# Attention by pairs of heads: q and k of two heads in one 128-row tile, scores as 64-row products on the two halves of the array

## The chip, the core and the metric

The kernel runs on one core of a Trainium2 chip. The core has a matrix engine (TensorE, PE in the profile, with its weight loads as PEld), a vector engine (VectorE, DVE), a scalar engine (ScalarE, ACT), a general engine (GpSimd, POOL) and a queue processor that starts transfers (SyncE, SP). The metric is the device time of one launch in microseconds (us); lower is better. Matmuls read two operands from the on-chip memory (SBUF): the weights (lhsT), which are loaded into the array, and the moving operand (rhs), which streams through it column by column; the result goes to PSUM, eight banks of 128 partitions x 512 fp32 values.

## The reference

Three stages run one behind the other on 1,792 tokens (4 batches x 448) with 768 features: causal attention with 12 heads of 64 per batch, a top-1 mixture of 8 experts (768 to 1024 to 768, ReLU), and a second feed-forward layer (768 to 2048 to 768 with h - tanh(h)). The part that matters here:

```
q, k, v: (4, 12, 448, 64) fp32
scores = (q @ k.T) / sqrt(64)
scores = where(causal mask, -1e9, scores)
scores = scores - max(scores, axis=-1)
attn   = exp(scores);  attn /= sum(attn, axis=-1) + 1e-9
out    = attn @ v                       # then (1792, 768)
expert = argmax(x @ w_gate); x -> prob * (relu(x @ w1[expert]) @ w2[expert])
x -> (h - tanh(h)) @ w_out, h = x @ w_in
```

## The kernel before

The attention works through 48 heads (4 batches x 12), the loop `for n in range(NHEAD + 2)` at L632. Products that need more precision than one pass in the 32-bit format fp32r gives are made from parts: x = hi + lo, where hi is x rounded to fp32r and lo the rest.

For each head three 128-row operand tiles and one tile of 65 rows exist. `q1` holds q hi in rows 0 to 63 and q lo in rows 64 to 127; `k1` holds k hi twice; `q2` holds q hi and, in row 64, minus the row maximum; `k2` holds k lo and a row of ones. So `k1` by `q1` is k hi (q hi + q lo) in one product of 128 rows, and `k2` by `q2` adds k lo q hi and subtracts the row maximum in one product of 65 rows (`attend`, L552 and L553). Scores come out with keys on partitions, in four blocks of 128 keys and 448, 320, 192 and 64 queries (the causal part). ACT takes the exponent (L554) into `pT`, POOL zeroes the half above the diagonal (L555).

The row maximum has to be known first. `rowmax` (L528) makes approximate scores with queries on partitions, again four blocks of up to 128 queries and 64 to 448 keys, and DVE takes mask and maximum in one instruction (L530, with a second, short one that reads the accumulator). `maxrow` (L540, L541) turns the four columns of maxima into a row of `q2`.

`turn` (L455, L459) turns q or k of two heads at once on PE (128 rows: the two heads), and ACT writes each head's half as hi; `turn_lo` (L468) makes lo on DVE, one instruction per head; `turn_dup` (L475) makes the second copies on ACT. `weigh` (L567) is the product with v in full fp32 (two records a call), `output` (L585 to L599) turns the result back and divides by the sum of the weights. Between these, `cv` converts blocks of the last layer's weights for later (L108 to L132: ACT, POOL, three DVE instructions, POOL), `pick`, `rank` and `choose` do the gate of a batch that is complete, and near the end `fetch0` and `gather` fetch the first expert's tokens.

Each engine runs its instructions in the order in which the loop writes them. Scores and maxima have two PSUM banks each (`ps_s`, `ps_a`), turned tiles two (`ps_t`), `pv` and `po` one each. The first head is handled apart by `begin` (L477). After the attention the experts start with L799.

Of the kernel before, what the change touches and what calls it, by code (L numbers as in the profile page):

```python
# [27 lines left out]
def fused_kernel(ctx, tc, q, k, v, wg, w1, w2, win, wout, out):  # L28
# [6 lines left out]
    CP = 112  # L35
# [168 lines left out]
    ps_a = ectx.enter_context(tc.tile_pool(name="ps_a", bufs=2, space=PSUM))  # L204
    ps_s = ectx.enter_context(tc.tile_pool(name="ps_s", bufs=2, space=PSUM))
# [162 lines left out]
    with ExitStack() as actx:  # L368
# [3 lines left out]
        xsp = actx.enter_context(tc.tile_pool(name="xsp", bufs=2))  # L372
        ps_p = actx.enter_context(tc.tile_pool(name="ps_p", bufs=1, space=PSUM))
        NQ = 7
# [7 lines left out]
        raw_t, ops_t, max_t, pt_t, ov_t, xs, tn_t = {}, {}, {}, {}, {}, {}, {}  # L382

        k2s = [ap1.tile([D + 1, S], F32R, name=f"k2_{i}") for i in range(NQ)]
        vs = [ap1.tile([KP, NKB, 2, D + 1], F32, name=f"v_{i}") for i in range(NV)]

# [9 lines left out]
        def load_v(i):  # L396
            b, hp = divmod(i, NP)
            v_sb = vs[i % NV]
            nf = S // KP
            for j in range(2):  # L400
                nc.sync.dma_start(out=v_sb[:, 0:nf, j, 0:D],
                                  in_=v[b, 2 * hp + j, 0:nf * KP].rearrange("(c p) d -> p c d", p=KP))
            if S % KP:
                nc.sync.dma_start(out=v_sb[0:S % KP, nf, :, 0:D],
                                  in_=v[b, 2 * hp:2 * hp + 2, nf * KP:].rearrange("j p d -> p j d"))
# [6 lines left out]
        load_qk(0)  # L412
        load_qk(1)
# [4 lines left out]
        mcs = [ap1.tile([KP, NKB], F32R, name=f"mcol{i}") for i in range(3)]  # L418
        pts = [ap1.tile([KP, NKB, S], F32, name=f"pT{i}") for i in range(2)]
        junk = ap1.tile([KP, S], BF16, name="junk")  # L420
        for t in k2s:
            nc.gpsimd.memset(t[D:D + 1].bitcast(F32), 1.0)
        for t in vs:
            nc.gpsimd.memset(t[:, :, :, D:D + 1], 1.0)
            if S % KP:
                nc.gpsimd.memset(t[S % KP:, NKB - 1], 0.0)
        for t in mcs:
            nc.gpsimd.memset(t.bitcast(F32), 0.0)
        for t in pts:
            if S % KP:  # L430
                nc.gpsimd.memset(t[S % KP:, NKB - 1, S - S % KP:], 0.0)
# [7 lines left out]
        def turn(i, z, pool=ps_t, tag="tp"):  # L439
            if i >= NPAIR:  # L440
                return
            q_sb, k_sb = raw_t[i]
            if z:
                for j in range(2):
                    n = 2 * i + j
                    q1 = ap2.tile([128, S], F32R, tag="q1", name="q1", bufs=NQ)
                    k1 = ap2.tile([128, S], F32R, tag="k1", name="k1", bufs=NQ)
                    q2 = ap2.tile([D + 1, S], F32R, tag="q2", name="q2", bufs=NQ)
                    ops_t[n] = (q1, k1, q2, k2s[n % NQ])
# [3 lines left out]
            pt = pool.tile([128, S], F32, tag=tag, name="tp")  # L453
# [3 lines left out]
            for j in range(2):  # L457
                q1, k1, q2, k2 = ops_t[2 * i + j]
                nc.scalar.copy(out=(k1 if z else q1)[0:D], in_=pt[j * D:(j + 1) * D])  # L459
            tn_t[i, z] = pt  # L460

        def turn_lo(i, z):
            if (i, z) not in tn_t:
                return
            pt = tn_t.pop((i, z))
            for j in range(2):
                q1, k1, q2, k2 = ops_t[2 * i + j]
                nc.vector.tensor_tensor(out=k2[0:D] if z else q1[D:], in0=pt[j * D:(j + 1) * D],  # L468
                                        in1=(k1 if z else q1)[0:D].bitcast(F32), op=ALU.subtract)

        def turn_dup(i, z, j):
            if i >= NPAIR:
                return
            q1, k1, q2, k2 = ops_t[2 * i + j]
            nc.scalar.copy(out=k1[D:] if z else q2[0:D], in_=(k1 if z else q1)[0:D].bitcast(F32))  # L475

        def begin():  # L477
            q_sb, k_sb = raw_t[0]
            pts = {}
            for j in range(2):  # L480
                for z, src in ((1, k_sb), (0, q_sb)):
                    pool, tag = (ps_p, ("po", "pv")[z]) if j else (ps_t, "tp")
                    pt = pool.tile([128, S], F32, tag=tag, name="pt0")
                    for c in range(NCH):
                        nc.tensor.transpose(pt[0:D, c * CP:(c + 1) * CP], src[:, c, j, :], ident[:CP, :CP])
                    pts[j, z] = pt[0:D]
                q1 = ap2.tile([128, S], F32R, tag="q1", name="q1", bufs=NQ)
                k1 = ap2.tile([128, S], F32R, tag="k1", name="k1", bufs=NQ)
                q2 = ap2.tile([D + 1, S], F32R, tag="q2", name="q2", bufs=NQ)
                ops_t[j] = (q1, k1, q2, k2s[j])  # L490
            raw_t.pop(0)
            for j in range(2):
                q1, k1, q2, k2 = ops_t[j]
                nc.scalar.copy(out=k1[0:D], in_=pts[j, 1])
                nc.vector.tensor_copy(k1[D:], k1[0:D].bitcast(F32))
                nc.scalar.copy(out=q1[0:D], in_=pts[j, 0])
                nc.vector.tensor_tensor(out=q1[D:], in0=pts[j, 0], in1=q1[0:D].bitcast(F32), op=ALU.subtract)
                if j == 0:
                    nc.scalar.copy(out=q2[0:D], in_=q1[0:D].bitcast(F32))
# [698 lines left out]
```

## Time and profile before

| | |
|---|---|
| time, median of 3 runs | 1141.39 us (1140.04 to 1143.49) |
| profiled execution | 1140.54 us, span from first to last instruction 1139.1 us |
| busy: PE, PEld, DVE, ACT, POOL | 95%, 86%, 69%, 57%, 37% of the span |
| attention | from 0 to about 291.8 us, where the first expert product starts |
| attention, 22.23 to 281.03 us | PE busy 236.27, DVE 228.19, ACT 214.38, POOL 129.62 of 258.80 us |

Busy time of a matmul counts from its start to the modelled end of its result, so neighbouring matmuls overlap in it; the distance between their starts says more on what one costs. An idle stretch has the instruction that ended it behind an arrow. A tile's name is that of the program, without the number: the tiles `q1`, `q2`, `k1`, `k2` all appear as q and k.

### The profile page before, as it was taken

To read this page: it belongs to the slowest core of one execution; us is meant where nothing else is said; L and a number is where in the kernel's file an instruction comes from. 1 tells how busy PE (TensorE), PEld (TensorE's weight loads), DVE (VectorE), ACT (ScalarE), POOL (GpSimd) and SP (SyncE) were. 2 spreads that over 40 slices of the span, in tenths; PEclk is the share of its full clock that TensorE was granted. 3 is DMA by queue.
4 is the path that set the end of the run, shared out by engine and by line. 5 is a ranking of instruction groups with operands and counts; after the bars stand their busy time and mean duration, and the time that the engine had idled before them with its cause. 6 is when DMAs were issued, how large, how long until landed. Compare 5 with 4: busy or idle time off the path is not lost. (4 is left out here: it accounts for less than half of the span.)

```text
span 1139.1 us, 22520 instructions
## 1 busy us (share of the span) xinstructions
PE 1077.2 (95%) x7019; PEld 980.6 (86%) x7019; DVE 782.7 (69%) x1958; ACT 649.6 (57%) x1415; POOL 417.1 (37%) x740
## 2 busy tenths in 40 slices
PE   6999899989899999998999899999999999999996
PEld 4676676766789888988889899999999999999996
DVE  5888999997822444617565599889999865556653
ACT  5888888887422544627565565555567634434442
POOL 5555454543314101011102245657674322222221
PEclk8999999999999999999999999999999999999999
DMA  7677676755451557718878353444656422331310
GB/s 154 169 192 178 171 171 164 176 132 159 147 153 43 174 165 245 250 57 283 261 250 289 127 190 132 132 159 164 206 178 230 167 85 83 111 105 64 112 52 33
DMA packets 151044, 179.75 MB, mean 158 GB/s; under 512 B 75392, under 2 KB 119936, under 8 KB 149120
## 3 DMA queue, kind: packets, MB, share of 16 engines
q1 hardware_dynamic: 144656, 148.30, 43.4%
q0 software_dynamic: 6256, 29.90, 7.9%
q8 instruction: 57, 0.93, 0.3%
q14 instruction: 75, 0.61, 0.2%
HBM read 263.49 MB, written 46.80 MB: 272 GB/s over the span
## 5 line engine op out<-in xcount | busy, mean ns | idle before, releaser
L1032 PE MATMUL ph<-yt,w1hi 128*128 128x256 f32 x1344 | 260.4, 284 | 3.4 <-ACTq L973 3.4
L1069 PE MATMUL po<-w2hi,gg 128*128 128x384 f32 x896 | 248.1, 338 | 2.3 <-DVE gg L151 2.3
L1032 PEld LDWEIGHTS ph<-yt,w1hi 128*128 128x128 f32 x1344 | 217.7, 192 | 3.7 <-ACTq L973 3.7
L1032 PE MATMUL ph<-yt,w1lo 128*128 128x256 f32 x672 | 190.5, 283 | 0.0
L1069 PEld LDWEIGHTS po<-w2hi,gg 128*128 128x128 f32 x896 | 164.2, 189 | 2.6 <-DVE gg L151 2.6
L1069 PE MATMUL po<-w2lo,gg 128*128 128x384 f32 x448 | 150.3, 336 | 0.0
L799 PE MATMUL ph<-w1hi,xt 128*128 128x512 f32 x432 | 145.0, 403 | 0.0
L1032 PEld LDWEIGHTS ph<-yt,w1lo 128*128 128x128 f32 x672 | 128.8, 192 | 0.0
L1050 DVE SCALAR_TENSOR_TENSOR g<-sq,g 128x256 f32<-128x256 f32 x224 | 111.4, 497 | 11.6
L567 PE MATMUL pv<-pT,v 128*65 128x64 f32 (+3 forms) x384 | 111.3, 391 | 0.2 <-POOL pT L555 0.2
L528 PE MATMUL pa<-k,q 128*128 128x448 f32 x192 | 88.9, 465 | 23.3 <-DVE q L468 17.9
L819 PE MATMUL py<-w2hi,hhi 128*128 128x384 f32 x288 | 100.7, 350 | 1.6 <-ACT hhi L149 1.6
L819 PE MATMUL py<-w2hi,hlo 128*128 128x384 f32 x288 | 98.2, 341 | 1.3 <-DVE hlo L151 1.3
L819 PE MATMUL py<-w2lo,hhi 128*128 128x384 f32 x288 | 97.8, 340 | 0.0
L799 PEld LDWEIGHTS ph<-w1hi,xt 128*128 128x128 f32 x432 | 82.7, 191 | 17.5
L530 DVE CUSTOM_DVE_ANT_0 junk<-pa,maskf 128x448 bf16<-128x448 f32 x192 | 80.2, 418 | 24.5 <-PE pa L528 6.5
L151 DVE TENSOR_TENSOR hlo<-tp,hhi 128x512 fp32r<-128x512 f32 x36 | 24.8, 689 | 104.0 <-ACTq L778 99.4
L109 POOL TENSOR_SCALAR cv_m<-cv_m 128x256 f32<-128x256 f32 (+3 forms) x82 | 83.1, 1013 | 28.2 <-ACT cv_m L108 23.1
L151 DVE TENSOR_TENSOR w2lo<-raw,w2hi 128x1536 fp32r<-128x1536 f32 x40 | 69.7, 1760 | 33.3 <-ACT w2hi L149 33.1
L528 PEld LDWEIGHTS pa<-k,q 128*128 128x128 f32 x192 | 35.1, 184 | 62.7 <-DVE q L468 26.2
L151 DVE TENSOR_TENSOR w1lo<-raw,w1hi 128x1536 fp32r<-128x1536 f32 (+1 forms) x47 | 68.6, 1480 | 26.2 <-ACT w1hi L149 25.3
L799 PE MATMUL ph<-w1lo,xt 128*128 128x512 f32 x216 | 86.1, 399 | 0.0
(675 smaller groups left out, 2340.6 us busy)
## 6 DMA issues: line engine op xcount, KB each, us to landing
raw<-in_moe_w_dram SPq DMA_DIRECT2D x148, 768.0 KB
raw<-win_dr POOLq DMA_DIRECT2D x72, 768.0 KB
raw<-wout_dr POOLq DMA_DIRECT2D x17, 768.0 KB
yt_dr<-yt SPq DMA_DIRECT2D x7, 1536.0 KB
yt<-yt_dr SPq DMA_DIRECT2D x7, 1536.0 KB
y_dr<-ysb POOLq DMA_DIRECT2D x18, 384.0 KB
cv_raw<-in_moe_w_out_dram SPq DMA_DIRECT2D x24, 256.0 KB
cv_raw<-in_moe_w_in_dram SPq DMA_DIRECT2D x24, 256.0 KB
```

What stands on the lines that cost most here:

```text
L109: nc.gpsimd.tensor_scalar(out=m, in0=m, scalar1=TINY * TINY, scalar2=None, op0=ALU.is_ge)
L151: eng.tensor_tensor(out=dlo, in0=src, in1=dhi.bitcast(F32), op=ALU.subtract)
L528: nc.tensor.matmul(pa[:nq, :w], lhsT=q1[:, q0:w], rhs=k1[:, :w], start=True, stop=True)
L530: nc.vector.tensor_tensor_reduce(out=junk[:nq, :w], in0=pa[:nq, :w], in1=maskf[:nq, m0:m0 + w], scale=1.0, scalar=-3.0e38, op0=ALU.add, op ...
L567: nc.tensor.matmul(pv[:, k0:], lhsT=vs[(n // 2) % NV][:, kb, n % 2, :], rhs=pt_t[n][:, kb, k0:], start=(kb == 0), stop=(kb == NKB - 1))
L799: nc.tensor.matmul(ph, lhsT=a[:, kk, :], rhs=w[:, kk, z * 512:(z + 1) * 512], start=(kk == 0 and n_ == 0), stop=(kk == KD - 1 and n_ == 2))
L819: nc.tensor.matmul(pys[z], lhsT=a[:, kk, :], rhs=w[:, kk, z * HALF:(z + 1) * HALF], start=(kk == 0 and n_ == 0), stop=(kk == KF - 1 and n_ ...
L1032: nc.tensor.matmul(ph, lhsT=w[:, kk, f * 128:(f + 1) * 128], rhs=yt[:, a, kk, :], start=(kk == 0 and n_ == 0), stop=(kk == KD - 1 and n_ = ...
L1050: nc.vector.scalar_tensor_tensor(out=g, in0=sq, scalar=float(c_), in1=g, op0=ALU.add, op1=ALU.mult)
L1069: nc.tensor.matmul(po_t[ub][tt][z], lhsT=gg[:, a, tt * 128:(tt + 1) * 128], rhs=w[:, f, z * HALF:(z + 1) * HALF], start=(f == 0 and n_ == ...
```

## The change

Two heads become one unit, a pair. `turn` still turns two heads at once, but its 128 rows (head 0 in rows 0 to 63, head 1 in rows 64 to 127) are kept as they are: ACT writes `qhi` or `khi` in one instruction, `turn_lo` writes `qlo` or `klo` in one, and `turn_dup`, `q1`, `q2`, `k1`, `k2` are gone. `half(t, j)` is head j's 64 rows of a tile. The scores of a block of keys are four products of 64 rows for each head: k hi q hi, k hi q lo, k lo q hi, and `one` by `mrow`, which subtracts the maximum; the two heads' products stand next to each other, one on rows 0 to 63 and one on rows 64 to 127, and write to two PSUM banks of one tile `ps`. `rowmax` is q hi by k hi alone, two products of 64 rows. One exponent and one mask instruction then do both heads. `ps` and `pa` are now one buffer of two banks each. The last block's weights are 128 columns, of which 64 are wanted (before 64). `maxrow` is done once for a pair. The start has no `begin`: it turns the first three pairs and takes the maxima of the first two before the loop, whose body is written out anew for a pair; what the loop did at head n (conversion, gate, fetches) is in `convert(n)` and `events(n)`.

```diff
-    ps_a = ectx.enter_context(tc.tile_pool(name="ps_a", bufs=2, space=PSUM))
-    ps_s = ectx.enter_context(tc.tile_pool(name="ps_s", bufs=2, space=PSUM))
...
+        ps_c = actx.enter_context(tc.tile_pool(name="ps_c", bufs=1, space=PSUM))
...
+        one = ap1.tile([KP, KP], F32R, name="one")
+        nc.vector.memset(one.bitcast(F32), 0.0)
+        for j in range(2):
+            nc.vector.memset(one[j * D:j * D + 1].bitcast(F32), 1.0)
...
-            for j in range(2):
-                q1, k1, q2, k2 = ops_t[2 * i + j]
-                nc.scalar.copy(out=(k1 if z else q1)[0:D], in_=pt[j * D:(j + 1) * D])
+            nc.scalar.copy(out=ops_t[i][2 * z], in_=pt)
...
-                nc.vector.tensor_tensor(out=k2[0:D] if z else q1[D:], in0=pt[j * D:(j + 1) * D],
-                                        in1=(k1 if z else q1)[0:D].bitcast(F32), op=ALU.subtract)
-
-        def turn_dup(i, z, j):
+            hi, lo = ops_t[i][2 * z:2 * z + 2]
+            nc.vector.tensor_tensor(out=lo, in0=tn_t.pop((i, z)), in1=hi.bitcast(F32), op=ALU.subtract)
+
+        def half(t, j):
+            return t[j * D:(j + 1) * D]
...
-            nc.tensor.matmul(pa[:nq, :w], lhsT=q1[:, q0:w], rhs=k1[:, :w], start=True, stop=True)
+            pa = ps_c.tile([KP, 2, 512], F32, tag="pa", name="pa")
+            for j in range(2):
+                nc.tensor.matmul(pa[:, j, :w], lhsT=half(qhi, j)[:, q0:q0 + KP], rhs=half(khi, j)[:, :w],
+                                 start=True, stop=True)
...
-            nc.tensor.matmul(ps[:nk, k0:], lhsT=k1[:, k0:k0 + nk], rhs=q1[:, k0:], start=True, stop=False)
-            nc.tensor.matmul(ps[:nk, k0:], lhsT=k2[:, k0:k0 + nk], rhs=q2[:, k0:], start=False, stop=True)
-            nc.scalar.activation(out=pT[:nk, kb, k0:], in_=ps[:nk, k0:], func=AF.Exp, scale=0.125)
+            w, o = S - k0, KO[kb]
+            p0, kk = KP - nk, k0 + nk - KP
+            ps = ps_c.tile([KP, 2, 512], F32, tag="ps", name="ps")
+            for n_, (a, m) in enumerate(((khi, qhi), (khi, qlo), (klo, qhi), (one, mrs[i % 2]))):
+                ks = slice(0, KP) if a is one else slice(kk, kk + KP)
+                for j in range(2):
+                    nc.tensor.matmul(ps[:, j, :w], lhsT=half(a, j)[:, ks], rhs=half(m, j)[:, k0:],
+                                     start=(n_ == 0), stop=(n_ == 3))
+            nc.scalar.activation(out=pT[p0:, :, o:o + w], in_=ps[p0:, :, :w], func=AF.Exp, scale=0.125)
...
+        for p in range(NPAIR + 2):
+            last = 2 * (p - 1)
+            attend(p, 0)
+            rowmax(p + 2, 3)
+            weigh(last, 0)
+            weigh(last, 1)
+            convert(2 * p)
+            attend(p, 1)
+            rowmax(p + 2, 2)
+            weigh(last, 2)
+            weigh(last, 3)
+            output(last - 1)
+            maxrow(p + 1)
+            events(2 * p)
+            attend(p, 2)
+            rowmax(p + 2, 1)
+            weigh(last + 1, 0)
+            weigh(last + 1, 1)
+            turn(p + 3, 1)
+            convert(2 * p + 1)
+            turn_lo(p + 3, 1)
+            attend(p, 3)
+            rowmax(p + 2, 0)
+            weigh(last + 1, 2)
+            weigh(last + 1, 3)
+            output(last)
+            turn(p + 3, 0)
+            turn_lo(p + 3, 0)
```

On PE, in the middle of the attention, the matmuls of one head stood so before (ps: scores, pa: approximate scores, pm: maxima turned, pv: product with v; the shape is that of the result; x4 is four instructions in a row):

```order
L552 MATMUL ps<-q_1424,k_1425 128x448
L553 MATMUL ps<-q_1426,k_3_178 128x448
L528 MATMUL pa<-k_1598,q_1597 128x448
L552 MATMUL ps<-q_1424,k_1425 128x320
L553 MATMUL ps<-q_1426,k_3_178 128x320
L540 MATMUL pm<-identr,mcol_205 1x128 x4
L567 MATMUL pv<-pT_208,v_184 65x448
L528 MATMUL pa<-k_1598,q_1597 128x320
L552 MATMUL ps<-q_1424,k_1425 128x192
L553 MATMUL ps<-q_1426,k_3_178 128x192
L552 MATMUL ps<-q_1424,k_1425 64x64
L553 MATMUL ps<-q_1426,k_3_178 64x64
```

In the change the same place holds, for two heads, four score products and one approximate product for each width, each twice (x2: the two halves), with the product with v behind each block:

```order
L503 MATMUL ps<-qhi,khi 128x448 x2
L503 MATMUL ps<-qlo,khi 128x448 x2
L503 MATMUL ps<-qhi,klo 128x448 x2
L503 MATMUL ps<-mrow_182,one 128x448 x2
L475 MATMUL pa<-khi,qhi 128x448 x2
L517 MATMUL pv<-pT_179,v_175 65x448
L517 MATMUL pv<-pT_179,v_175 65x320
L503 MATMUL ps<-qhi,khi 128x320 x2
L503 MATMUL ps<-qlo,khi 128x320 x2
L503 MATMUL ps<-qhi,klo 128x320 x2
L503 MATMUL ps<-mrow_182,one 128x320 x2
L475 MATMUL pa<-khi,qhi 128x320 x2
```

So for a width two heads took four score products and two approximate ones before, and take eight and two now, all of them of 64 rows.

On DVE, at the end of a head, the maxima (ISA), the lo parts (L468) and the output stood so before (mcol: columns of maxima; rs, x_sb, tl: output):

```order
L530 ISA junk,mcol_206<-pa,maskf 128x192
L530 ISA mcol_206 128x1
L530 ISA junk,mcol_206<-pa,maskf 64x64
L530 ISA mcol_206 64x1
L468 TENSOR_TENSOR q_2326<-tp,q_2326 64x448
L468 TENSOR_TENSOR q_2329<-tp,q_2329 64x448
L587 TENSOR_SCALAR rs<-po 112x4
L588 RECIPROCAL rs<-rs 112x4
L590 TENSOR_TENSOR x_sb<-po,rs 112x4x64
L598 TENSOR_TENSOR tl<-po,rs 112x32
L530 ISA junk,mcol_206<-pa,maskf 128x448
```

At the end of a pair in the change:

```order
L462 TENSOR_TENSOR klo<-tp,khi 128x448
L479 ISA junk,mcol_181<-pa,maskf 64x64
L479 ISA mcol_181 64x1
L479 ISA junk,mcol_181<-pa,maskf 64x64
L479 ISA mcol_181 64x1
L536 TENSOR_SCALAR rs<-po 112x4
L537 RECIPROCAL rs<-rs 112x4
L539 TENSOR_TENSOR x_sb<-po,rs 112x4x64
L547 TENSOR_TENSOR tl<-po,rs 112x32
L462 TENSOR_TENSOR qlo<-tp,qhi 128x448
L479 ISA junk,mcol_180<-pa,maskf 128x448
```

The lo parts of a pair are two instructions of 128 rows where there were four of 64; the maxima and the output are as many as before, the maxima of the two heads now side by side.

At the start of the program PE of the change turns pairs and takes maxima before the first score product (tp: turned q or k):

```order
L453 MATMUL tp<-ident,q_sb 128x112 x4
L475 MATMUL pa<-khi,qhi 128x448 x2
L475 MATMUL pa<-khi,qhi 128x320 x2
L475 MATMUL pa<-khi,qhi 128x192 x2
L475 MATMUL pa<-khi,qhi 128x64 x2
L488 MATMUL pm<-identr,mcol_180 65x128 x4
L453 MATMUL tp<-ident,k_sb 128x112 x4
L453 MATMUL tp<-ident,q_sb 128x112 x4
L503 MATMUL ps<-qhi,khi 128x448 x2
```

These rows begin with the q of the second pair; the k and q of the first pair and its four pairs of maxima stand ahead of them. Before, the first score product stood behind the first head's four maxima.

## Rows read from the trace of the kernel before

**Rows 1.** Stretches: length, busy PE, PEld, DVE, ACT, POOL, granted clock, DMA share, GB/s.
```profile
22.23:281.03 258.80, 236.27 (x1661) 179.44 (x1661) 228.19 (x830) 214.38 (x501) 129.62 (x305) 0.97 0.67 168
149.87:160.49 10.62, 9.77 (x76) 7.74 (x74) 9.47 (x37) 9.33 (x23) 5.66 (x15) 1.00 0.64 171
160.49:170.93 10.44, 9.78 (x76) 7.82 (x74) 9.49 (x34) 9.33 (x23) 5.09 (x13) 1.00 0.73 181
```

**Rows 2.** Timeline of DVE: start, duration, engine, line, operation.
```profile
155.46 1.28 DVE L468 TENSOR_TENSOR q<-tp,q 64x448 fp32r<-64x448 f32 x2
156.76 0.16 DVE L587 TENSOR_SCALAR rs<-po 112x4 f32<-112x4 f32 x1
...
157.61 0.61 DVE L530 CUSTOM_DVE_ANT_0 junk<-pa,maskf 128x448 bf16<-128x448 f32 x1
```

**Rows 3.** Waits from 100 to 200 us: total, times, longest.
```profile
PE pa L528 <- DVE q L468: 6.2, 8, 1.0
```

**Rows 4.** Timeline of PE, two heads from 149.87 us.
```profile
149.87 0.45 PE L552 MATMUL ps<-q,k 128*128 128x448 f32 x1
150.16 0.36 PE L553 MATMUL ps<-q,k 65*128 65x448 f32 x1
150.36 0.37 PE L528 MATMUL pa<-k,q 128*128 128x448 f32 x1
150.57 0.31 PE L552 MATMUL ps<-q,k 128*128 128x320 f32 x1
150.72 0.31 PE L553 MATMUL ps<-q,k 65*128 65x320 f32 x1
150.87 0.41 PE L540 MATMUL pm<-identr,mcol 128*1 128x128 f32 x4
151.11 0.92 PE L567 MATMUL pv<-pT,v 128*65 128x448 f32 x2
...
152.02 0.26 PE L552 MATMUL ps<-q,k 128*128 128x192 f32 x1
152.11 0.27 PE L553 MATMUL ps<-q,k 65*128 65x192 f32 x1
152.22 0.20 PE L552 MATMUL ps<-q,k 128*64 128x64 f32 x1
152.25 0.22 PE L553 MATMUL ps<-q,k 65*64 65x64 f32 x1
152.30 0.60 PE L455 MATMUL tp<-ident,q_sb 112*128 112x112 f32 x4
...
154.63 0.45 PE L552 MATMUL ps<-q,k 128*128 128x448 f32 x1
...
156.13 0.47 PE L528 MATMUL pa<-k,q 128*128 128x448 f32 x1 [0.85 <-DVE q L468]
```

**Rows 5.** Groups of DVE and ACT by shape, 100 to 200 us: busy, mean ns, idle before.
```profile
L468 DVE TENSOR_TENSOR k<-tp,k 64x448 fp32r<-64x448 f32 x18 | 11.1, 618 | 0.2
L475 ACT CAST k<-k 64x448 fp32r<-64x448 f32 x18 | 9.3, 561 | 0.2
L554 ACT ACTIVATE pT<-ps 128x448 f32<-128x448 f32 x17 | 9.2, 541 | 1.4 <-PE ps L553 1.1
L554 ACT ACTIVATE pT<-ps 64x64 f32<-64x64 f32 x18 | 3.7, 208 | 0.0
```

**Rows 6.** Timeline of PE, start of the program.
```profile
5.72 0.95 PE L485 MATMUL pt<-ident,q_sb 112*64 112x112 f32 x4
...
22.23 0.72 PE L552 MATMUL ps<-q,k 128*128 128x448 f32 x1
```

**Rows 7.** Timeline of PE, end of the attention.
```profile
276.84 0.45 PE L552 MATMUL ps<-q,k 128*128 128x448 f32 x1
...
290.46 0.72 PE L232 MATMUL tp<-identr,xg 128*128 128x128 f32 x6 [2.73 <-DMA xg<-x_dr,idx]
...
291.79 0.48 PE L799 MATMUL ph<-w1hi,xt 128*128 128x512 f32 x1
```

More of the change, by code (lines that the diff above doesn't have):

```diff
@@ L410, in load @@
                 load_v(i)
-        load_qk(0)
-        load_qk(1)
+        for i in range(3):
+            load_qk(i)
         maskf = ap1.tile([KP, S], BF16, name="maskf")
@@ L437, in fused_kernel, with turn @@
         nc.gpsimd.memset(zrow, 0.0)
-        def turn(i, z, pool=ps_t, tag="tp"):
-            if i >= NPAIR:
+        def turn(i, z):
+            if not 0 <= i < NPAIR:
                 return
@@ L477, in begin @@
[L477 to L499, printed above, removed]
-                    for c in range(NKB - 1, -1, -1):
-                        rowmax(0, c)
-                nc.vector.tensor_tensor(out=k2[0:D], in0=pts[j, 1], in1=k1[0:D].bitcast(F32), op=ALU.subtract)
-            maxrow(0)
-            nc.scalar.copy(out=q2[0:D], in_=q1[0:D].bitcast(F32))
-            turn(1, 1)
-            turn_dup(1, 1, 0)
-            turn_dup(1, 1, 1)
-            for c in range(NKB - 1, -1, -1):
-                attend(0, NKB - 1 - c)
-                rowmax(1, c)
-                if c == NKB - 2:
-                    turn(1, 0)
-                if c == 1:
-                    turn_lo(1, 0)
-            for j in range(2):
-                turn_dup(1, 0, j)
-            turn_lo(1, 1)
@@ L679, in fused_kernel @@
             if n == N0 + 9:
-                oh0 = early()
+                e0_t[1] = early()
             if n == N0 + 10:
-                fetch0(oh0)
+                fetch0(e0_t[1])
             for i in range(3 * NG1):
@@ L686, in fused_kernel @@
                     if i % 3 == 2:
-                        raw2(i // 3, w2[bass.ds(e0, 1)].rearrange("e k f -> (e k) f"))
+                        raw2(i // 3, w2[bass.ds(e0_t[0], 1)].rearrange("e k f -> (e k) f"))
             if n == NHEAD:
                 xturn(0)
-        store(NHEAD - 1)
+        load_v(1)
+        cv.load(nc.sync)
+        cv.load(nc.sync)
+        load_v(2)
+        load_v(3)
+        for i in range(3):
+            for z in (1, 0):
+                turn(i, z)
+            for z in (1, 0):
+                turn_lo(i, z)
+            if i < 2:
+                load_qk(i + 3)
+            if i == 2:
+                nc.gpsimd.tensor_copy(wid[:, :, 0:D + 1],
+                                      ident[:D + 1, 0:D + 1].unsqueeze(1).to_broadcast([D + 1, H, D + 1]))
+            for c in range(NKB - 1, -1, -1):
+                rowmax(i if i < 2 else -1, c)
+            if i == 1:
+                maxrow(0)
+        for p in range(NPAIR + 2):
[26 more added lines that the diff above has]
+            turn_lo(p + 3, 0)
+            if p + 5 < NPAIR:
+                load_qk(p + 5)
+            if p + 4 < NPAIR:
+                load_v(p + 4)
+            events(2 * p + 1)
+        for n in range(NHEAD - 3, NHEAD):
+            store(n)
         assert cv.stored == len(cv.jobs)
```

132 lines of the change are left out of this document (44 added, 88 removed).

## The prediction

> **What bounds the kernel now.** Only the attention is touched, so I read its stretches first. In two ordinary pairs of heads (10.62 and 10.44 us, mean 10.53) PE, DVE and ACT are all busy for about nine tenths, DVE with 9.47 and 9.49 us [rows 1]. Which of them sets the pace a share does not tell, so I went to the timelines. DVE has no hole: one instruction starts within 0.02 us of the end of the one before [rows 2]; what its busy time lacks to the stretch is the hand-over between instructions that need each other's result. PE does have a hole: at 156.13 it has waited 0.85 us for a lo part of DVE, and from 100 to 200 us it loses 6.2 us in 8 such waits [rows 3, 4]. A head without that wait takes 154.63 - 149.87 = 4.76 us, the next one 5.86 (the next score product of 448 columns is at 160.49, where the second stretch begins) [rows 1, 4]. So DVE is the bound at 10.53 us a pair, and PE, let run, would need 2 x 4.76 = 9.52.
>
> Over the long stretch from head 1 to head 47 a pair takes 258.8 / 23 = 11.25 us [rows 1]: about 0.7 more than an ordinary pair, for the gate, the first slow heads and the early expert work, most of which is DVE's.
>
> **DVE, ACT and POOL.** Four lo parts of 64 rows become two of 128. By their rows a lo part takes 0.62 us, and the 64 rows lie side by side, so 128 should take the same: DVE loses 2 x 0.62 = 1.24 us a pair [rows 5] and would stand at 10.53 - 1.24 = 9.3. Maxima, output and conversion keep their number and shape. ACT loses four copies of 0.56 and two casts of 0.53 (I price a cast like the copy beside it), one of two turns of maxima, and the fixed part of four exponents: 541 ns for 448 columns and 208 for 64 give 0.87 ns a column and 0.15 us fixed [rows 5]. That is 2.2 + 1.1 + 0.5 + 0.6 = 4.4 of 9.3 us. ACT was not the bound; what this buys is cover for the new single buffers. POOL does as many elements in half the instructions and is busy for half the time anyway [rows 1].
>
> **PE, the term that decides.** From the distances between starts one head's scores and maxima cost 0.29 + 0.20 + 0.21 + 0.15 + 0.15 (two score products of 448, one approximate, two of 320), 0.09 + 0.11 + 0.03 + 0.05 (192 and 64), and for three approximate products that stand between products with v 0.14 + 0.09 + 0.03, priced like score products of their width: 1.54 us, 3.08 a pair. One turn of maxima, 151.11 - 150.87 = 0.24, goes [rows 4]. What stays on PE is 9.52 - 3.08 - 0.24 = 6.2 us a pair.
>
> What comes is, for each width, five times two products of 64 rows. The trace of before has no 64-row product, so the price has two bounds. If the halves run at the same time, two cost what one costs: 0.20, 0.15 and 0.09 us for 448, 320 and 192 columns. Each also loads its own 128 weight columns; two products of 64 columns with 64 weight columns start 0.03 us apart [rows 4], so I estimate 0.06 for 128 columns and no pair of products under 0.12. Five times (0.20 + 0.15 + 0.12 + 0.12) = 2.95 us. The first product behind one in fp32 costs 0.09 more (0.29 against 0.20 at 149.87): four blocks, 0.36. Leaving and entering the 64-row form happens eight times a pair; the nearest row is the step from 128 to 64 weight columns, 0.11 after a product that else takes 0.09, and back 0.05 where 0.03 is expected [rows 4]: 0.02 a time, 0.16. In all 6.2 + 2.95 + 0.36 + 0.16 = 9.7. With weight loads wholly hidden it is 9.1. If the halves do not run together, it is five times 2 x (0.20 + 0.15 + 0.09 + 0.06) = 5.0, and PE needs 6.2 + 5.0 + 0.5 = 11.7.
>
> I take the first, because the two products use different rows of the array and different banks, and because products with disjoint data already overlap by all but the stream of columns here. The Trainium skill speaks for it too, in "TensorE: Matmul & The Clock Gate", Part 3 (Packing small matmuls): products on different row groups run concurrently, with 3.07 times measured for four of 32 rows. By that rule two halves would cost nearly one, as in my sum; no row of before shows it for fp32r.
>
> **Single buffers.** `ps` is free again when the exponent of the block has run: for two heads of 448 columns 0.15 + 896 x 0.87 ns = 0.93 us, and between two score blocks PE has products with v of 448 and 320 columns, (448 + 320) x 4 passes at 0.20 us per 448 = 1.4 us, so it hides; without that cover each block would add up to 0.9. `pa` is free after two maxima on DVE (0.61 each [rows 2], some 1.4 us with their readings), and the PE work from one approximate product to the next is 1.4 us and more everywhere except between the second and third block, where it is about 2 us of product with v, output and turned maxima: DVE stays fed, with little spare. The weights of v, the loads and the conversion are the same work.
>
> **Start and end.** Before the loop PE now turns three pairs and takes eight pairs of maxima, each waiting for the single `pa`. The last input of the first pair is there at 5.72 [rows 6]. Then 1.0 us of turning (0.95 in the same row) and 1.0 of cast and start, eight maxima of 4 us with four round trips of 0.5, 2 us of turning, the same maxima again, and 2 us for the third pair: 5.7 + 2 + 6 + 2 + 6 + 2 = 23.7; I take 23 for the first score product of pair 0. Before, at 22.23, head 1 starts [rows 6], so the change begins about one head behind.
>
> At the end the distance from the first score product of pair 23 (276.84) to the first expert product (291.79) is 15 us, of which 2.73 is a wait for the gathered tokens [rows 7]. The change keeps the order of gather, turn and last outputs; I leave these 15 us as they are.
>
> **The sum.** An ordinary pair: PE 9.7 and DVE 9.3 lie close, so 9.7; the extras, mostly DVE's, add 0.6 of their 0.7 since DVE has 0.4 to spare: 10.3. Pair 23 then starts at 23 + 23 x 10.3 = 260 against 276.84: 17 us earlier, and the experts and the last layer move with it: the transfers of the stretch would take a share of 0.67 x 11.25 / 10.3 = 0.73 of the DMA engines instead of 0.67 [rows 1], still not the bound. Profiled execution: 1140.5 - 17 = 1123.5; the median of the runs is 0.9 above that execution, so 1124. A pair of 10.0 to 10.6 and a start at 23 give 253 to 267, thus 24 to 10 us: with 2 us for the start, 1114 to 1133.
>
> **Rivals.** First, the halves run one behind the other: the change then doubles the columns of the scores. PE at 11.7 becomes the bound, DVE waits, and its extras mostly vanish in that wait: 11.8 a pair, 23 + 23 x 11.8 = 294, 18 us later, 1159; with part of the weight loads hidden, down to 1144. It decides as soon as a pair exceeds (276.84 - 23) / 23 = 11.0 us, which is when the second half of each two costs more than about 60% of a product. For it: nothing here shows overlap of fp32r halves, and weight loads double. Against: different rows and banks.
>
> Second, the change of form empties the array each time. A 64-column product takes 0.20 us from start to end and the next starts 0.03 later [rows 4], so emptying would cost 0.17: eight times 1.4 instead of 0.16, PE 10.9, a pair 11.1 with some extras, 23 + 23 x 11.1 = 278, about 1143; a half of that cost gives 1134. Against it stand the 0.02 us of the steps to 64 weight columns and back. The Trainium skill states such a drain in "TensorEngine Tiling (Array Packing)", Tiling Modes, Key Properties: changing the mode drains the engine. The trace agrees only in so far as the step is not free; for a change of rows no row shows it.
>
> Third, as a smaller one inside the likeliest: PE reaches 9.1, DVE stays the bound at 9.3 and the pair takes 9.9, giving about 1114.
>
> **Chances.** Halves together, small step (1114 to 1133): 0.58. Emptying or half overlap (1134 to 1148): 0.16. One behind the other (1144 to 1164): 0.26. This kernel's runs spread by 0.3%, so 1138 to 1145 counts as no change. Faster by more: 0.57 of the first and 0.05 of the second, 0.62. No change: 0.01, 0.07 and 0.03, 0.11. Slower: 0.27. The range from 1113 to 1154 leaves out a twentieth below and about an eighth above, in the upper half of the first rival.
>
> **What would show it.** Score products of the two halves starting in pairs, with 0.2 us from one pair of 448 columns to the next; a pair of heads in 9.7 to 10.3 us; L462 at 0.62 us for 128 rows and two of them a pair; ACT busy for about half; first score product at 23 us and first expert product near 275. Wrong would be two products 0.2 us apart each, PE without holes at 11 us and more, holes of 0.17 us where the products with v begin and end, or DVE waiting for `pa`.

## The result, and the profile after

| | before | after |
|---|---|---|
| time, median | 1141.06 us (1140.04 to 1143.49) | 1131.02 us (1128.68 to 1132.68), 4 runs |
| ratio to before, 95% interval | | 0.9907 [0.988, 0.9935] |
| profiled execution, span | 1140.54, 1139.1 us | 1132.68, 1131.2 us |
| busy: PE, DVE, ACT, POOL | 95%, 69%, 57%, 37% | 96%, 67%, 50%, 36% |
| first score product of the last pair | 276.84 us [rows 7] | 259.43 us |
| first expert product | 291.79 us [rows 7] | 282.23 us |

Faster by 10 us; 17 were forecast. The last pair starts 17.4 us earlier, as forecast; at the first expert product 9.6 us of that are left. Busy time by stretches of the changed kernel (all pairs but the first and the last; the last pair to the first expert product; an ordinary pair), the counterpart of [rows 1]:

```profile
core 0: us, PE busy (x) PEld busy (x) DVE busy (x) ACT busy (x) POOL busy (x), PEclk, DMA share, GB/s
...
33.05:259.43 226.38, 225.57 (x1833) 161.18 (x1833) 190.58 (x736) 124.89 (x241) 113.61 (x206) 1.00 0.69 184
259.43:282.23 22.80, 19.54 (x124) 13.69 (x123) 12.12 (x37) 10.32 (x20) 7.68 (x10) 0.79 0.48 154
157.58:167.80 10.22, 10.22 (x86) 7.35 (x85) 8.52 (x34) 5.70 (x11) 4.97 (x10) 1.00 0.60 144
```

An ordinary pair takes 10.2 us in place of 10.53, and PE is busy in all of it; DVE is idle for 1.7 us of it and ACT for 4.5. The waits for DVE's lo part [rows 3] are gone. The stretch from 259.43 is another matter: 22.8 us where 14.95 stood before, with PE idle for 3.3 us and a mean granted clock of 0.79.

PE's timeline of the pair from 157.58, the counterpart of [rows 4]:

```profile
start us, us, engine line op out<-in xcount [idle before <-releaser]
...
157.58 0.49 PE L503 MATMUL ps<-qhi,khi 64*128 64x448 f32 x2
157.90 0.37 PE L503 MATMUL ps<-qlo,khi 64*128 64x448 f32 x2
158.12 0.37 PE L503 MATMUL ps<-qhi,klo 64*128 64x448 f32 x2
158.32 0.37 PE L503 MATMUL ps<-mrow,one 64*128 64x448 f32 x2
158.52 0.37 PE L475 MATMUL pa<-khi,qhi 64*128 64x448 f32 x2
158.82 1.50 PE L517 MATMUL pv<-pT,v 128*65 128x448 f32 x4
160.26 0.41 PE L503 MATMUL ps<-qhi,khi 64*128 64x320 f32 x2
...
162.44 0.44 PE L488 MATMUL pm<-identr,mcol 128*65 128x128 f32 x4
162.81 0.36 PE L503 MATMUL ps<-qhi,khi 64*128 64x192 f32 x2
```

Two products of 448 columns (x2, one for each head) follow the two before them after 0.20 us, the price of one before the change. The first of a block takes 0.32 to the next, and from the last to the product with v there are 0.30 where 0.20 would be its stream. The turn of maxima of two heads takes 162.81 - 162.44 = 0.37; one head's took 0.24 [rows 4].

The end of the attention in the same execution, PE's timeline, POOL's, and stretches of 4 us (columns as above):

```profile
268.33 1.80 PE L517 MATMUL pv<-pT,v 128*65 128x448 f32 x6
272.27 0.33 PE L517 MATMUL pv<-pT,v 128*65 128x64 f32 x2 [2.14 <-POOL pT L506]
...
274.48 3.64 PE L517 MATMUL pv<-pT,v 128*65 128x448 f32 x8
...
280.74 1.74 PE L534 MATMUL po<-wid,ov 65*112 65x73 f32 x8 [1.11 <-DVE tl L547]
282.23 0.77 PE L780 MATMUL ph<-w1hi,xt 128*128 128x512 f32 x1
```

```profile
266.64 1.21 POOL L219 DMA_INDIRECT xg<-x_dr,idx  x1 [0.18 <-issue]
267.88 0.41 POOL L506 TENSOR_SCALAR_AFFINE_SELECT pT<-pT 128x256 f32<-128x256 f32 x1
271.93 0.29 POOL L506 TENSOR_SCALAR_AFFINE_SELECT pT<-pT 64x128 f32<-64x128 f32 x1 [3.64 <-DMA xg<-x_dr,idx]
```

```profile
268.00:272.00 4.00, 2.13 (x11) 1.00 (x9) 2.06 (x6) 1.26 (x3) 0.36 (x2) 1.00 0.94 355
272.00:276.00 4.00, 3.73 (x19) 2.70 (x20) 1.94 (x6) 2.42 (x5) 1.40 (x3) 0.58 0.04 10
276.00:280.00 4.00, 3.63 (x15) 2.64 (x13) 1.35 (x5) 1.56 (x3) 0.23 (x1) 0.50 0.61 197
```

POOL issues the gather of the first expert's tokens at 266.64 and then holds the last mask of the last pair until the gathered tokens have landed. PE needs that mask to finish the product with v and waits 2.14 us; behind the wait the granted clock is 0.58 and 0.50 (its level of 1.2 GHz), so eight records of products with v take 3.64 us. In the kernel before, four masks ran right behind the gather without a wait; POOL's timeline there:

```profile
283.41 1.21 POOL L221 DMA_INDIRECT xg<-x_dr,idx  x1 [0.18 <-issue]
284.64 0.96 POOL L555 TENSOR_SCALAR_AFFINE_SELECT pT<-pT 128x128 f32<-128x128 f32 x4
```

Its wait for the gather stood at the very end, at PE's turn of the tokens (2.73 us [rows 7]): the mask's wait for the same gather takes the place of that one. The written programs show the difference. POOL's instructions of the changed kernel (241, 242) and of before (301, 302) behind the gather; DMASW0 is the gather's queue:

```
241 L506 AFFINE_SELECT pT_179<-pT_179 128x2x128 [waits Activation_49]
242 L506 AFFINE_SELECT pT_179<-pT_179 64x2x64 [waits DMASW0_49,Activation_49,Pool_49]
...
301 L555 AFFINE_SELECT pT_208<-pT_208 128x128 [waits Activation_49] x3
302 L555 AFFINE_SELECT pT_208<-pT_208 64x64 [waits Activation_49]
```

Wait and clock are not all. The stretch from the last pair's first score product to the first expert product, in the kernel before, in a second run of the changed kernel and in one with the gather issued earlier (both from the side-by-side runs in the experiments below), all three at the full clock (columns as above):

```profile
276.84:291.79 14.95, 12.05 (x97) 9.35 (x96) 9.44 (x30) 9.63 (x24) 8.23 (x13) 1.00 0.60 175
258.69:277.72 19.03, 15.62 (x123) 10.86 (x123) 11.82 (x37) 10.22 (x20) 7.32 (x10) 1.00 0.55 178
257.55:275.03 17.48, 15.47 (x124) 10.97 (x123) 11.83 (x37) 10.12 (x20) 8.10 (x10) 1.00 0.61 197
```

PE has 3.6 us more to do in it than before. `weigh` and `output` now follow the scores by a pair where they followed by a head, so behind the last pair's first score product stand the products with v of four heads (32 records) and five outputs, where it was three heads (24 records) and four outputs. One head's products with v take 1.76 us and an output 0.76 (in the run with the earlier gather they start at 267.39 and 269.15, what follows at 269.91). So 2.5 of the 17.4 us at the last pair's start are work that was moved behind it, not saved. The rest of the 3.6 is about what the last pair's own blocks cost more, by estimate: four changes into the 64-row form and back at 0.31 us (measured below), less one turn of maxima of 0.24.

### The profile page after: what moved, and what is told of

It is laid out like the page before. It is cut to its first block, busy times and chain, and to the rows that moved or that the text cites. A ratio compares the mean times of both kernels' runs of the same rounds, so it can differ in the third digit from the quotient of the medians.

```text
span 1131.2 us, 22514 instructions
## 1 busy us (share of the span) xinstructions
PE 1085.8 (96%) x7299; PEld 973.8 (86%) x7299; DVE 757.5 (67%) x1915; ACT 560.5 (50%) x1153; POOL 403.3 (36%) x634
## 5 line engine op out<-in xcount | busy, mean ns | idle before, releaser
L517 PE MATMUL pv<-pT,v 128*65 128x64 f32 (+3 forms) x384 | 106.1, 400 | 2.1 <-POOL pT L506 2.1
L479 DVE CUSTOM_DVE_ANT_0 junk<-pa,maskf 128x448 bf16<-128x448 f32 (+1 forms) x192 | 80.4, 419 | 12.9 <-PE pa L475 8.7
L1050 PEld LDWEIGHTS po<-w2lo,gg 128*128 128x128 f32 x448 | 84.9, 190 | 0.0
L517 PEld LDWEIGHTS pv<-pT,v 128*65 128x65 f32 x384 | 46.0, 139 | 44.7 <-issue 28.1
```

The costliest lines, as they stand in the source:

```text
L479: nc.vector.tensor_tensor_reduce(out=junk[:nq, :w], in0=pa[:nq, j, :w], in1=maskf[:nq, m0:m0 + w], scale=1.0, scalar=-3.0e38, op0=ALU.add, ...
L517: nc.tensor.matmul(pv[:, k0:], lhsT=vs[i % NV][:, kb, j, :], rhs=pts[i % 2][:, j, KO[kb]:KO[kb + 1]], start=(kb == 0), stop=(kb == NKB - 1))
L1050: nc.tensor.matmul(po_t[ub][tt][z], lhsT=gg[:, a, tt * 128:(tt + 1) * 128], rhs=w[:, f, z * HALF:(z + 1) * HALF], start=(f == 0 and n_ == ...
```

## The experiments

Every edit is made to the changed kernel. Where durations in the trace decide, one profiled execution was taken; where a time decides, several executions beside the kernel before. Diffs are shown in part; `...` marks what is left out.

**Do the halves run at the same time?** Two runs. The first gives both heads' products the same 64 rows; head 1's scores and maxima are then head 0's.

```diff
-lhsT=half(qhi, j)[:, q0:q0 + KP], rhs=half(khi, j)[:, :w]
+lhsT=half(qhi, 0)[:, q0:q0 + KP], rhs=half(khi, 0)[:, :w]
...
-lhsT=half(a, j)[:, ks], rhs=half(m, j)[:, k0:]
+lhsT=half(a, 0)[:, ks], rhs=half(m, 0)[:, k0:]
```

> The 64-row score and maximum products of both heads all take the operands of head 0, so that all stand on rows 0 to 63 of the array (head 1's scores and maxima are replaced by head 0's); same number of products, columns and form changes. Theory (two products run side by side because they use different rows): the 20 pairs of products of a pair no longer overlap, and each of the distances 0.20, 0.15, 0.11 and 0.115 us doubles or nearly so, 2.0 to 2.9 us more a pair: 12.2 to 13.1 us a pair, 1180 to 1200 us. Rival (the product is cheaper whatever the rows, or something else than the array sets the distance): 10.2 us a pair and 1128 to 1133 us. If the pair becomes longer here but stayed as it was with the four products of one head ahead of the other's, the order in the program does not matter and the rows do.

Measured: 1220.55 us, a pair 176.19 - 163.15 = 13.04 us. PE's timeline of this run:

```profile
163.66 0.57 PE L503 MATMUL ps<-qlo,khi 64*128 64x448 f32 x2
164.07 0.56 PE L503 MATMUL ps<-qhi,klo 64*128 64x448 f32 x2
```

0.41 us from one two products to the next, twice 0.20, and a pair 2.84 us longer, five times (0.20 + 0.15 + 0.11 + 0.11). With the same number of products and columns on the same 64 rows nothing is left of the overlap. (The whole execution lost 89 us, more than 24 x 2.84 = 68; part of the rest is at the start, where pair 0 begins at 25.37 and pairs 0 and 1 take 14.5 and 15.6.) The second run writes the four score products of head 0 first, then the four of head 1:

```diff
-            for n_, (a, m) in enumerate(((khi, qhi), (khi, qlo), (klo, qhi), (one, mrs[i % 2]))):
-                ks = slice(0, KP) if a is one else slice(kk, kk + KP)
-                for j in range(2):
+            for j in range(2):
+                for n_, (a, m) in enumerate(((khi, qhi), (khi, qlo), (klo, qhi), (one, mrs[i % 2]))):
+                    ks = slice(0, KP) if a is one else slice(kk, kk + KP)
```

> The same score products in another order: four of head 0, then four of head 1, so that neighbours use the same 64 rows; the approximate products stay side by side. Theory that two halves run at the same time only when they stand next to each other: eight products of 448 columns take 8 x 0.2 = 1.6 us instead of 0.8, a pair of heads 10.2 + 4 x (0.20 + 0.15 + 0.08 + 0.06) = 12.1 us, the time about 1131 + 23 x 1.9 = 1175. Rival that the engine finds the other half by itself whatever the order, or that the gain is not from overlap: a pair stays within 0.3 us of 10.2.

Measured: 1128.28 us, a pair 10.24 us. PE's timeline of this run:

```profile
156.63 0.49 PE L503 MATMUL ps<-qhi,khi 64*128 64x448 f32 x2
156.95 0.37 PE L503 MATMUL ps<-qlo,khi 64*128 64x448 f32 x2
```

The adjacency theory falls. The records still show the products in twos: head 1's first starts beside head 0's first, though three others of head 0 stand between them in the program. So in these records neither half waits for the other's place in the program.

**Is PE alone the bound of a pair?** Once PE's work is cut, once DVE's. The first leaves the products with `one` out, so the exponents are taken of scores that the maximum isn't subtracted from:

```diff
-            for n_, (a, m) in enumerate(((khi, qhi), (khi, qlo), (klo, qhi), (one, mrs[i % 2]))):
+            for n_, (a, m) in enumerate(((khi, qhi), (khi, qlo), (klo, qhi))):
...
```

> The product that subtracts the row maximum (one by mrow) is left out of every score block, so the exponents are not shifted; the maxima are still computed. Theory that TensorE alone sets the pace of a pair now: 0.20 + 0.15 + 0.11 + 0.115 = 0.58 us less a pair, 9.6 us, about 13 us less time. Rival that VectorE is as close a bound as I forecast (9.3 to 9.7): the pair falls by less than 0.3 us.

Measured: 1118.14 us, a pair 163.14 - 153.45 = 9.69. The second takes the maxima of head 0 alone (head 1's are left out):

```diff
-            for j in range(2):
+            for j in range(1):
                 nc.vector.tensor_tensor_reduce(out=junk[:nq, :w], in0=pa[:nq, j, :w], in1=maskf[:nq, m0:m0 + w],
```

> VectorE takes the maxima of head 0 alone (half of its reductions are left out, so head 1's scores are not shifted); TensorE's work is the same. Theory (in an ordinary pair TensorE alone is the bound): VectorE falls by about 1.5 us a pair and the pair stays at 10.2 us; 1129 to 1132 us, a little less if the pairs that the gate's work lengthens are VectorE's. Rival (VectorE's round trips still set part of the pair, TensorE's records only look full): 9.5 us a pair or less, 1115 us.

Measured: 1122.21 us, and the ordinary pair stays at 153.58 - 143.41 = 10.17, with DVE busy for 7.1 of it. So in an ordinary pair PE is the bound, and taking 0.6 us of products away shortens it by 0.5. The time nevertheless missed its expectation by 7 us: the first score product comes at 20.02 in place of 23.36 (the maxima ahead of it are half as many), the last pair's start another 2 us earlier (the five pairs that took 10.6 to 10.8 us take 10.2 to 10.4, so those DVE did hold up), and the half clock of the end didn't appear in this execution (below).

**What does a change of form cost?** The approximate products stand behind the first product with v and no longer beside the scores, so that PE enters and leaves the 64-row form eight times a pair in place of four; all work is kept.

```diff
             attend(p, 0)
-            rowmax(p + 2, 3)
             weigh(last, 0)
+            rowmax(p + 2, 3)
             weigh(last, 1)
...
```

The three other blocks are edited alike.

> The approximate products stand between the two products with v of their block instead of right behind the score products: the same instructions, and TensorE enters and leaves the 64-row form eight times a pair instead of four. Theory that entering and leaving cost about 0.1 us each (the distance from the last 64-row product to the product with v is 0.30 where the stream takes 0.20): 8 more changes of form, 0.8 us a pair, 11.0 us, 18 us more time. Rival that the 0.5 us that TensorE needs above my sum lie in the fp32 products and turned maxima and not in the form: the pair stays within 0.3 us of 10.2.

Measured: 1150.68 us, a pair 11.45 us, 1.24 more: 0.31 for each way in and out, half as much again as expected. PE's timeline of this run:

```profile
159.02 0.37 PE L503 MATMUL ps<-mrow,one 64*128 64x448 f32 x2
159.32 0.97 PE L517 MATMUL pv<-pT,v 128*65 128x448 f32 x2
160.22 0.47 PE L475 MATMUL pa<-khi,qhi 64*128 64x448 f32 x2
160.62 0.75 PE L517 MATMUL pv<-pT,v 128*65 128x320 f32 x2
```

The two products of 448 columns at 160.22 are alone between 128-row products and take 0.40 where their stream is 0.20. The Trainium skill, "TensorEngine Tiling (Array Packing)", Tiling Modes, Key Properties, says that changing the mode drains the engine; the rows agree that a change isn't free, and put it at 0.31 / 2 = 0.155 us. A rival is the change between fp32r and full fp32, since products with v are in fp32. The kernel before settles it: there an approximate product of 128 rows in fp32r stood alone between products with v, too.

```profile
106.33 0.70 PE L567 MATMUL pv<-pT,v 128*65 128x320 f32 x2
106.87 0.36 PE L528 MATMUL pa<-k,q 128*128 128x192 f32 x1
107.06 0.49 PE L567 MATMUL pv<-pT,v 128*65 128x192 f32 x2
```

From one product with v to the next there are 0.73 us (0.63 at 152.74), where the streams are 4 x 0.14 + 0.09 = 0.66 at 0.20 us for 448 columns (four streams a product with v, as the prediction reckons): at most 0.07 more. In this run the same distance is 160.62 - 159.32 = 1.30, where the streams are 4 x 0.20 + 0.20 = 1.00. So most of the 0.31 goes with the 64 rows.

**The end of the attention.** The gather is moved from the end of pair 23 to right behind its first score block, ahead of the pair's other masks on POOL.

```diff
-            if n == N0 + 10:
-                fetch0(e0_t[1])
...
             attend(p, 0)
+            if 2 * p == N0 + 10:
+                fetch0(e0_t[1])
             rowmax(p + 2, 3)
```

> The first expert's tokens are fetched right behind the first score block of pair 23 instead of behind the turned maxima, some 3 us earlier; nothing else changes. Theory: the 7.9 us lost at the end (22.8 us from pair 23's first score product to the first expert product, against 15.0 before the change) come from the last mask instruction on GpSimd, which waits for that transfer, and from the half clock that follows the 2.1 us hole on TensorE. Then the last mask waits at most 1 us, the clock stays at 1.0 until the experts begin, the 22.8 us become 15 to 17, and the time falls by 5 to 8 us to 1123 to 1126. Rival: the end is long because outputs and early expert work queue on VectorE and ScalarE; then the stretch stays above 20 us and the time at 1129 to 1132.

Measured: 1125.62 us (1122.91 to 1127.72), ratio to before 0.9881 [0.9861, 0.9902]. From the last pair's start (257.79) to the first expert product there are 17.46 us. PE's timeline of this run:

```profile
259.76 0.44 PE L325 MATMUL r_p<-f_oh,sel 112*128 112x1 f16 x12 [0.88 <-DVE f_oh L318]
...
270.65 1.91 PE L517 MATMUL pv<-pT,v 128*65 128x448 f32 x8
...
275.25 0.48 PE L780 MATMUL ph<-w1hi,xt 128*128 128x512 f32 x1
```

No wait for the mask, and the eight records take 1.91 us where they took 3.64. What the edit costs is a wait of 0.88 us for the gate's one-hot, which PE now meets sooner. To part the wait from the clock, the next run keeps the late gather and fills the wait with eleven products of no use:

```diff
             weigh(last, 2)
+            if p == NPAIR:
+                fill = ps_t.tile([128, S], F32, tag="tp", name="fill")
+                for _ in range(11):
+                    nc.tensor.matmul(fill, lhsT=identr, rhs=ops_t[NPAIR - 1][2], start=True, stop=True)
             weigh(last, 3)
```

> The kernel after the change with eleven 448-column products of no use put ahead of the last of pair 23's weighing, where TensorE waits 2.14 us for the mask that waits for the gather. Theory (the wait itself costs about 2 us, and the half clock behind it the other 5 to 6): the clock stays at its upper level, the stretch from the last mask to the first expert product falls from 10 to 5 or 6 us, and the execution is 3 to 6 us faster than the changed kernel, 1125 to 1128 us. Rival (the clock falls for another reason, or the slow products there wait for transfers): within 1 us of the changed kernel.

Measured: 1127.32 us (1126.71 to 1128.74), ratio 0.9901 [0.9868, 0.9934]. PE's timeline of this run:

```profile
268.35 2.53 PE L648 MATMUL fill<-khi,identr 128*128 128x448 f32 x11
271.22 0.33 PE L517 MATMUL pv<-pT,v 128*65 128x64 f32 x2 [0.34 <-POOL pT L506]
...
272.68 1.91 PE L517 MATMUL pv<-pT,v 128*65 128x448 f32 x8
...
277.27 0.47 PE L784 MATMUL ph<-w1hi,xt 128*128 128x512 f32 x1
```

With PE kept at work the clock stayed up there, and from the last mask to the first expert product it took 277.27 - 271.22 = 6.05 us in place of 282.23 - 272.27 = 9.96. But the ratio is that of the changed kernel, 0.9907, within either interval: a gain that the profile shows and the time doesn't. The other profiles explain it. Behind the same wait the eight records took 2.99 us without the maximum products and 3.64 with eight form changes, but 1.91 with the halves apart and with half the maxima. There the half clock came in some executions only, so that it stayed away here can't be put down to the fill. The changed kernel and the earlier gather were therefore run once more, side by side:

> The changed kernel once more, beside the earlier gather on one chip. Theory (the 2 us wait at the last mask is in every execution, the half clock behind it in some): a profile with the wait; the slow stretch behind it, 10 us from the last mask to the first expert product, or the quick one, 6 us; the times of the executions spread by some 4 us. Rival (the half clock always follows the wait): 10 us again.

> The earlier gather once more, on the chip of the run before. Theory: 2 us (the wait alone) to 6 us (wait and half clock) below the changed kernel, 4 in the median. Rival (what it gains at the end of the attention is lost again in the expert work behind it): within 1 us of the changed kernel.

Measured: 1128.36 us (1127.16 to 1128.59) for the changed kernel, ratio 0.9904 [0.9876, 0.9932]; 1122.84 us (1120.93 to 1124.04) for the earlier gather, ratio 0.9851 [0.982, 0.9881]: 5.5 us apart. PE's timeline of the changed kernel in this run:

```profile
271.67 0.33 PE L517 MATMUL pv<-pT,v 128*65 128x64 f32 x2 [2.29 <-POOL pT L506]
...
273.12 1.91 PE L517 MATMUL pv<-pT,v 128*65 128x448 f32 x8
...
277.72 0.47 PE L780 MATMUL ph<-w1hi,xt 128*128 128x512 f32 x1
```

The wait is there (2.29), the slow stretch isn't: 6.05 us to the first expert product, and 277.72 - 258.69 = 19.03 from the last pair's start. So the end costs 19.0 or 22.8 us by the clock, 17.5 with the gather early. Of the 3.6 us between the two profiled spans 1.1 lie ahead of the last pair's start, 1.6 in the end and 0.9 behind it; there the granted clock of the first 10 us of experts is 0.83 in the changed kernel, as in the kernel before, and 1.00 with the gather early (in its first run, too).

**A version that beats both.** Fewer changes of form should pay where PE is the bound. The blocks of 192 and 64 columns fit into one tile; put directly behind each other they save one way in and out a pair. On top of the earlier gather:

```diff
             attend(p, 2)
+            attend(p, 3, 256)
             rowmax(p + 2, 1)
+            rowmax(p + 2, 0, 256)
...
-            attend(p, 3)
-            rowmax(p + 2, 0)
...
```

> The earlier gather together with the two last score blocks of a pair (192 and 64 columns a head) in one shared tile and directly behind each other, so that the 64-row form is entered and left three times a pair and not four. Theory (one way in and out costs about 0.3 us, TensorE is the bound): 9.9 us a pair in place of 10.2, about 7 us less than with the earlier gather alone, 1117 to 1121 us. Rival (the two blocks share a buffer now, so the wait for ScalarE's exponents takes the gain): 1125 to 1130 us.

Measured: 1202.76 us (1195.99 to 1208.97), ratio 1.0548 [1.051, 1.0587], far worse than even the rival. PE's timeline of this run:

```profile
167.00 0.30 PE L510 MATMUL ps<-qhi,khi 64*128 64x64 f32 x2 [0.58 <-ACT pT L512]
...
168.66 0.30 PE L482 MATMUL pa<-khi,qhi 64*128 64x64 f32 x2 [0.87 <-DVE mcol L486]
168.89 2.82 PE L524 MATMUL pv<-pT,v 128*65 128x448 f32 x4
```

The second block's products wait for the exponent and the maximum of the first block, which read the same tile and stand ahead of them in the program; and behind the two waits the four records with v take 2.82 us where 1.50 was usual. The mend is an order: in `attend` and `rowmax` the products of both blocks first, then what reads them.

```diff
-            attend(p, 2)
-            rowmax(p + 2, 1)
+            attend(p, (2, 3))
+            rowmax(p + 2, (1, 0))
...
```

> As the run with the shared block (earlier gather, the two last score blocks of a pair in one shared tile, the 64-row form entered three times a pair), but all products of both blocks stand ahead of the first exponent and of the first reduction in the program, so that nothing that reads the shared tile stands between its two blocks. Theory (the shared block lost its time to the two round trips of 0.58 and 0.87 us and the half clock behind them, and one way in and out of the form costs 0.3 us): no wait between the blocks, 9.9 us a pair, 1117 to 1121 us, 5 to 8 below the earlier gather alone. Rival (the longer 64-row stretch brings the same waits in another place, for example in front of the next block or the next maxima): 10.2 us a pair or more, 1125 us or more.

Measured: 1114.67 us (1112.45 to 1116.87), ratio 0.9783 [0.9768, 0.9799]. Its stretch of one pair, and PE's timeline where the blocks meet:

```profile
163.05:172.94 9.89, 9.89 (x85) 7.38 (x85) 8.90 (x38) 5.79 (x12) 4.71 (x10) 1.00 0.74 182
```

```profile
158.79 0.27 PE L507 MATMUL ps<-mrow,one 64*128 64x192 f32 x2
158.90 0.22 PE L507 MATMUL ps<-qhi,khi 64*128 64x64 f32 x2
```

The pair is 0.3 us shorter, as the cost of one way in and out said, and the last pair starts 5.6 us earlier than in the first run of the earlier gather (252.17 against 257.79). The time lies 2 us below the expectation, and the whole gain over the earlier gather (0.9783 against 0.9881 and 0.9851) is larger than those 5.6 us. Against the profile of that run the first expert product came 4.3 us earlier (270.92 against 275.25), and 5.6 us less were needed behind it, in code that the edit doesn't touch. That part was not followed; between the two runs of the earlier gather, one kernel, it differs by 2.7 us already. Last, the maxima ahead of pair 0 alternate between two tiles:

```diff
-                rowmax(i if i < 2 else -1, (c,))
+                rowmax(i if i < 2 else -1, (c,), "pa" if c % 2 else "ps")
...
```

> The run before this one, and the maxima of the first two pairs, ahead of the first score product, alternate between two PSUM tiles in place of one, so that the next block's products need not wait for the reduction of the last. Theory (at the start TensorE and VectorE wait for each other in turn, holes of 0.5 to 0.7 us on VectorE three times in each of the two pairs): the first score product 3 to 5 us earlier than 23.2 and the execution as much, 1113 to 1117 us. Rival (something else, such as the operands of the second pair, sets the start): within 1 us of the run before.

Measured: 1110.44 us (1108.66 to 1111.98), ratio 0.9747 [0.9733, 0.9761], the first score product at 19.27 in place of 23.16, and the time 4.2 us less than in the run before, as expected from there. This one beats both kernels, the changed one by some 18 us.

## Why the prediction was right or wrong

**Right: the halves overlap.** Two 64-row products cost what one costs: 0.20, 0.15, 0.11 and 0.11 us (forecast 0.20, 0.15, 0.12, 0.12). On the same rows they cost twice as much. The Trainium skill's rule for packed products ("TensorE: Matmul & The Clock Gate", Part 3) thus holds here for 64 rows in fp32r too.

**Right: DVE, ACT and the single buffers.** A lo part of 128 rows takes 0.62 us; the waits for it are gone; ACT is busy for half the span; within the pairs from 33 to 259 us PE waits 0.6 us in all for maxima in `pa`, and not for `ps`.

**Right in the sum, not in its terms: the pair.** Pair 0 starts at 23.36 (forecast 23), pair 23 at 259.43 (260), an average of 10.26 (10.3). But an ordinary pair is 10.2 and not 9.7, and the extras are 0.1 and not 0.6: two errors that cancel, which is luck. DVE is busy for 8.5 and idle for 1.7 us a pair; how much it needs with its waits, forecast at 9.3, the runs bound only from above, by the pair of 9.69. Of PE's 0.5, entering and leaving was mis-sized: 0.36 + 0.16 = 0.52 stood in the sum, the runs show 4 x 0.31 = 1.24. The turn of maxima adds 0.13, the products' stream takes 0.08 off. That is 0.77 too much, so the 6.2 us that stay must be some 0.25 less than reckoned. This was not taken apart.

**Half right: the second rival.** It made a change of form cost 0.17 us, against 0.02 in the sum; 0.155 was measured. It erred in what that adds up to, a pair of 11.1: it kept 0.36 for the first product of a block beside the change of form (the measured 0.31 holds both), took over the 6.2, and let 0.2 of extras remain on top.

**Wrong: "I leave these 15 us as they are."** This is the step that failed. The distance from the last pair's start to the first expert product is 22.8 us in the profile that the result came with and 19.0 in the repeat. The order of the steps was kept, as the prediction said, but their number behind the last pair's start was not: 15.62 us of PE's work in the repeat in place of 12.05, 2.5 of it since a pair's products with v and outputs now lag behind the scores, and about 1.0 for the form of the last pair's blocks. The waits came to 2.29 for the mask and 1.12 for `tl` in place of 2.73 for the tokens and 0.16: 0.5 more. Together that is 19.0 - 14.95 = 4.1. The remaining 3.8 of the result's profile are the half clock. The order of the program on PE and POOL, with what each instruction waits for, would have shown the work and the wait beforehand, not the clock.

With the gather early the kernel runs at 0.9881 and 0.9851 of before, 1124 to 1128 us against the 1141 of the result, so it comes near the 1124 that was forecast. That does not make the forecast right: it had left 2.73 us of wait for the gather in the 15 us, and the earlier gather takes that wait away. Its 17.48 us are 15.47 of work, 0.90 for the one-hot and 1.11 for `tl`. The kernel before was not run with an earlier gather, so how much of the 5.5 us it would have gained as well is not shown.

## What to carry to other kernels

Two products of 64 rows on the two halves of the array cost what one costs; what they cost besides is each step between the 64-row and the 128-row form, so put as many as possible behind each other, with everything that reads their tile written after the last of them. Read the end of a stretch as closely as its middle. Count what stands behind the last unit when the units grow: here 2.5 us of PE's work were only moved there. And look at what each instruction there waits for: here a mask waits for a gather that it has no data from. Last, judge a wait of 2 us on TensorE by the rows behind it as well, since the clock may fall there.

## What the runs showed of the hardware that was not expected

- Products on the two halves need not be neighbours in the program: with three products of the same half between them they still started together, and the pair took 10.24 us (13.04 on the same rows).
- A step between the 64-row form and 128-row products costs 0.155 us, on average of the two ways (11.45 us a pair with eight ways in and out, 10.2 with four, 9.89 with three).
- Behind a wait of 2.1 to 2.9 us TensorE's granted clock fell to 0.50 in some executions and not in others (the eight records with v took 3.64, 3.64 and 2.99 us behind 2.14, 2.57 and 2.92, but 1.91 behind 2.07, 2.26 and 2.29); in the changed kernel's first profile that cost 3.9 us up to the first expert product. A shorter wait can have it, too: behind 0.91 us for the one-hot the next four records with v took 2.60 us in the run with block behind block (start at 254.44) and 1.48 behind the same wait in the last run (249.73). What decides between them is open.
